# Turning v on TensorE by two transposes instead of selection matmuls, with its cast on GpSimd, in a linear-attention and soft-MoE kernel

## The chip, the cores and the metric

The kernel runs on one core of a Trainium2 chip. The metric is the time of one launch on the device in microseconds (us); lower is better. The core's engines work side by side, each through its own instructions in the order of the program: TensorE (PE in the profile; PEld is its loading of weights), VectorE (DVE), ScalarE (ACT), GpSimd (POOL) and SyncE (SP), which issues most of the loads. The transfers themselves run on sixteen DMA engines that all the issuing queues share.

## The reference

Two parts follow each other. The first is a linear attention with a decaying state, for a batch B of 4, 8 heads H, 768 tokens S and a head width D of 48:

```python
for t in range(S):
    kt, vt, rt = (k[:, :, t], v[:, :, t], r[:, :, t])
    cur = np.einsum('bhd,bhe->bhde', u[None] * kt, vt)
    y[:, :, t] = np.einsum('bhd,bhde->bhe', rt, state + cur)
    state = w[None, :, :, None] * state + np.einsum('bhd,bhe->bhde', kt, vt)
```

Its result becomes x, 3072 tokens of width 384. The second part is a soft mixture of experts with 8 experts of 4 slots each and an inner width of 1024. The logits are x @ phi. A softmax over the tokens mixes tokens into slots, each expert applies its w1, a maximum with zero and its w2 to its four slots, and a softmax over the slots mixes the results back into tokens. All inputs and the output are float32.

## The kernel before

**Units and iterations.** A unit m is one batch and two heads, so there are 16. A unit's 768 tokens are worked in two halves of three chunks of 128 tokens; the main loop runs i from -5 to 31, and iteration i belongs to unit mu = i // 2, half i % 2 ("odd" is the second half). The recurrence is rewritten in chunks: within a chunk, scores of keys against queries are masked to the past and multiplied by v; between chunks a state is carried in Mb. The powers of the decay w are multiplied into k and r beforehand, by tables W that tt (VectorE) and ex (ScalarE's exp) make during the first iterations.

**How k and r arrive.** In SBUF a partition holds six consecutive tokens (J = 6) of each head. scale multiplies k (j = 0) or r (j = 1) of unit m by its table and casts to bfloat16, on VectorE for m = 0 and on GpSimd for all others; three buffers kr_t take the results. t_pe transposes these six blocks on TensorE into T0 or T1, and t_evac on ScalarE copies them to kT or rT, putting the tokens in order as it does. b_pe and b_evac turn kT back, so that kn has tokens on partitions.

**How v arrives.** v is loaded by half: a partition holds three consecutive tokens (JV = 3) of each half, in pieces of 576 bytes. v_cast casts a unit to bfloat16 (v_bf), on GpSimd for m = 0 and on ScalarE for the others. v_pe brings a half's tokens in order by nine matmuls with the stationary selection matrix Q3, which v_evac copies out of the bank Vb as vn:

```python
for c in range(L):
    for j in range(JV):
        o = C * c - j + JV - 1
        O(pe.matmul(Vb[:, c * P2:(c + 1) * P2], Q3[:, o:o + C], vb[:, :, g, j, :],
                    start=(j == 0), stop=(j == JV - 1)))
```

**Order within an iteration.** The function O keeps the order written in the program for every engine. Iteration i issues a_pe and mask_f for half i+1 (scores, and VectorE's mask into AT), y_pe and y_evac for half i, v_pe and v_evac for half i+2, m_pe and z_evac for half i+1 (state, and VectorE's Z and dv), then VectorE's prod_f in even iterations or b_pe and b_evac in odd ones. GpSimd gets scale(mu+3, 0) in odd iterations and scale(mu+2, 1) in even ones. Then follow t_pe and t_evac of unit mu+2 (k in even, r in odd iterations), and v_cast(mu+2) in even ones. For batches that are complete, route adds the logits and the dispatch in three parts. mask_f reads the bank Ab, z_evac reads Mb, and prod_f reads T1 and kT.

**Loads.** SyncE issues k, r and v of batch 0 in pieces of two heads, then batch 1 likewise, phi, and batch 2 in three large transfers. One half of the first k piece is issued by ScalarE. Batch 3 reuses batch 0's buffer and is issued at iteration 3. The expert weights are issued by GpSimd at points of the loop given by a dictionary from iteration to number of transfers, the first right after a small copy that waits for k of batch 3:

```python
W_AT = {12: 1, 13: 1, 14: 1, 15: 1, 17: 1, 19: 1, 20: 1, 22: 1, 23: 1, 25: 1, 26: 5}
...
if i == min(W_AT):
    O(pool.tensor_copy(guard[:], raw_of(0, B - 1)[:, 0:1]))
```

The eight w1 matrices have memory of their own (w_all in the profile). Those of w2 go where batches 1 and 2 lay. After the loop come the last routing, the experts (L628 for w1, L665 for w2) and the output in eight transfers.

Of the kernel before, what the change touches and what calls it, by code (L numbers as in the profile page):

```python
# [9 lines left out]
def kernel(  # L10
# [13 lines left out]
    B, H, S, D = r.shape  # L24
    C = 128
    nC = S // C
# [17 lines left out]
    JV = T // C  # L44

    f32 = mybir.dt.float32
    bf = mybir.dt.bfloat16
# [11 lines left out]
    wk = ctx.enter_context(tc.tile_pool(name="wk", bufs=3))  # L59
# [14 lines left out]
    def raw_of(which, b):  # L74
        return raw[b % NR][:, which * RW:(which + 1) * RW]
# [3 lines left out]
    Ab = psb.tile([128, 2, 512], f32, name="Ab")  # L79
# [3 lines left out]
    Vb = psb.tile([128, 512], f32, name="Vb")  # L83
# [17 lines left out]
    phi_f = late[:, 128:128 + nM * ES]  # L101
# [7 lines left out]
    O(act.dma_start(out=wu3[0:4, :, 0:D], in_=w.rearrange("(q e) d -> q e d", e=2)))  # L109
    O(act.dma_start(out=wu3[4:8, :, 0:D], in_=u.rearrange("(q e) d -> q e d", e=2)))  # L110
    O(dve.memset(warm, 0.0))
    O(dve.memset(one_f, 1.0))
    zt = cst.tile([128, nQ, 3, P2], f32, name="zt")
    O(dve.memset(zt[:], 0.0))

    def load_kr(which, src, b, h0, h1):
        O(sp.dma_start(out=raw_of(which, b).rearrange("p (h x) -> p h x", h=H)[:, h0:h1, :],
                       in_=src[b, h0:h1].rearrange("h (p j) d -> p h (j d)", j=J)))

    def load_v(b, h0, h1):  # L120
        O(sp.dma_start(out=raw_of(2, b).rearrange("p (h x) -> p h x", h=H * G)[:, h0 * G:h1 * G, :],
                       in_=v[b, h0:h1].rearrange("h (g p j) d -> p (h g) (j d)", g=G, j=JV)))

    def load_batch(b, step, h=0):
        for h0 in range(h, H, step):
            load_kr(0, k, b, h0, h0 + step)
            load_kr(1, r, b, h0, h0 + step)
            load_v(b, h0, h0 + step)
# [1 line left out]
    O(sp.dma_start(out=RK[:, 0, :], in_=k[0, 0].rearrange("(p j) d -> p (j d)", j=J)))  # L130
    load_kr(1, r, 0, 0, 2)
    load_v(0, 0, 2)
    load_batch(0, 2, 2)
    load_batch(1, 2)
    O(sp.dma_start(out=phi_f, in_=moe_phi.rearrange("(p mo) s -> p (mo s)", mo=nM)))
    load_batch(2, H)

    def load_w(n, y0=0, y1=nF):
        if n < E:
# [18 lines left out]
    Q3 = cst.tile([128, QW], bf, name="Q3")  # L158
# [17 lines left out]
    ident = cst.tile([128, 128], bf, name="ident")  # L176
# [21 lines left out]

    tt(0, 0)
    tt(1, 0)  # L200
    spread(Vb, P2, H * D)
    ex(0, 0)
    ex(1, 0)
    wT = cst.tile([128, nQ], f32, name="wT")
# [18 lines left out]
    phi_b = acc[:].bitcast(bf)[:, 0:nM * ES]  # L223
    guard = cst.tile([128, 1], f32, name="guard")
    st = {}


    def scale(m, j):
# [28 lines left out]
        O(dve.tensor_copy(kn[:].rearrange("p c t -> p (c t)"), T0[:, 0:S]))  # L257

    def prod_f(m):
        pr = wk.tile([128, S], bf, name="prod", bufs=2)  # L260
        st["prod", m] = pr
        O(dve.tensor_mul(pr[:].rearrange("p (s j) -> p s j", j=J),  # L262
                         T1[:, 0:S].rearrange("p (j s) -> p s j", j=J),
                         st["kT", m][:].rearrange("p (s j) -> p s j", j=J)))


    def v_cast(m):
        b, q = divmod(m, nQ)
        vb = wk.tile([128, 2, G, JV, D], bf, name="v_bf", bufs=2)
        st["vb", m] = vb  # L270
        out, src = vb[:].rearrange("p h g j d -> p (h g j d)"), raw_of(2, b)[:, 2 * q * G * JV * D:2 * (q + 1) * G * JV * D]
        if m == 0:
            O(pool.tensor_copy(out, src))
        else:
            O(act.copy(out, src))  # L275


    def at(i):
        m, g = divmod(i, G)
        b, q = divmod(m, nQ)  # L280
        return m, b, q, g, b * G + g

    def v_pe(i):
        m, b, q, g, n = at(i)
        vb = st["vb", m]
        for c in range(L):
            for j in range(JV):
                o = C * c - j + JV - 1
                O(pe.matmul(Vb[:, c * P2:(c + 1) * P2], Q3[:, o:o + C], vb[:, :, g, j, :],  # L289
                            start=(j == 0), stop=(j == JV - 1)))  # L290

    def v_evac(i):
        vn = wk.tile([128, L, 2, D], bf, name="vn", bufs=3)
        st["v", i] = vn
        O(act.copy(vn[:].rearrange("p c e d -> p (c e d)"), Vb[:, 0:L * P2]))  # L295

    def a_pe(i):
        m, b, q, g, n = at(i)
# [168 lines left out]
            xt_ev(*ch[s])  # L467

    pend = []
    W_AT = {12: 1, 13: 1, 14: 1, 15: 1, 17: 1, 19: 1, 20: 1, 22: 1, 23: 1, 25: 1, 26: 5}  # L470
    T_AT = {-4: [(tt, 0, 1), (tt, 1, 1), (ex, 0, 1), (tt, 0, 2)], -3: [(ex, 1, 1), (ex, 0, 2)],
            -1: [(tt, 1, 2), (ex, 1, 2)], 0: [(tt, 0, 3), (ex, 0, 3)], 1: [(tt, 1, 3), (ex, 1, 3)]}
    Z_AT = {-3: 0, -1: 1, 1: 2, 2: 3}
# [25 lines left out]
    for i in range(-5, nH):  # L499
        mu, odd = divmod(i, 2)  # L500
# [10 lines left out]
        if 0 <= i < nH:  # L511
            y_pe(i)
            y_evac(i)
        if 0 <= i + 2 < nH:
            v_pe(i + 2)
            v_evac(i + 2)
        if 0 <= i + 1 < nH:
            m_pe(i + 1)
            z_evac(i + 1)
# [30 lines left out]
        if i in Z_AT:  # L550
            q = Z_AT[i]
# [12 lines left out]
        if i == 6:  # L564
            for mi in range(nM):
                for j in range(nM):
                    o = C * mi - j + nM - 1
# [3 lines left out]
                                start=(j == 0), stop=(j == nM - 1)))  # L571
# [123 lines left out]
    i = 0  # L695
# [44 lines left out]
```

The softmax here doesn't subtract the row's maximum and nothing guards it: scores larger than these inputs give would overflow.

## Time and profile before

| what | value |
|---|---|
| median of 13 runs | 121.8 us (121.13 to 122.4) |
| the profiled execution | 122.4 us |
| span of its instructions | 120.6 us |
| TensorE busy | 104.2 us (86%) |
| VectorE busy | 96.6 us (80%) |
| ScalarE busy | 83.8 us (69%) |
| GpSimd busy | 59.5 us (49%) |
| GpSimd's scalings of k and r (L233) | 30, 1425 ns each |
| v's selection matmuls (L289) | 288, 18.6 us busy |
| v's copies out of Vb (L295) | 32, 418 ns each |
| v's casts on ScalarE (L275) | 15, 677 ns each |
| v's cast on GpSimd (L273) | 1, 1027 ns |
| issue of one weight transfer on GpSimd (L140) | 591 ns |

The times come from one execution recorded by the hardware profiler. Matmuls overlap one another, so a matmul's mean duration is longer than the distance between two of them, and a TensorE that is busy all the time need not be at its peak; the distance between starts in the timeline is the better price. In the list of costly groups each row gives the line of the code, the engine and operation, what is written from what, the shape, the count, the busy time with the mean of one, and the idle time of the engine just before these instructions. The page's slices cut the span into 40 equal parts and show the busy share of each in tenths. In the rows of DMA queues stand the packets, the megabytes and the share of sixteen engines' time: q1 carries what SyncE issues, q0 what GpSimd issues.

### The profile page before, as it was taken

To read this page: it belongs to the slowest core of one execution; us is meant where nothing else is said; L and a number is where in the kernel's file an instruction comes from. 1 tells how busy PE (TensorE), PEld (TensorE's weight loads), DVE (VectorE), ACT (ScalarE), POOL (GpSimd) and SP (SyncE) were. 2 spreads that over 40 slices of the span, in tenths; PEclk is the share of its full clock that TensorE was granted. 3 is DMA by queue.
4 is the path that set the end of the run, shared out by engine and by line. 5 is a ranking of instruction groups with operands and counts; after the bars stand their busy time and mean duration, and the time that the engine had idled before them with its cause. 6 is when DMAs were issued, how large, how long until landed. Compare 5 with 4: busy or idle time off the path is not lost.

```text
span 120.6 us, 4336 instructions
## 1 busy us (share of the span) xinstructions
PE 104.2 (86%) x1797; PEld 83.8 (70%) x1797; DVE 96.6 (80%) x187; ACT 83.8 (69%) x183; POOL 59.5 (49%) x70
## 2 busy tenths in 40 slices
PE   5896997799999999999999999999998998896000
PEld 1356886588888888888888898898785596783000
DVE  6889989999999999899999899999964430399000
ACT  4359668799788898988997997999792520298000
POOL 7337713599999999978686596101000000011100
PEclk9999999999999999999999999999999999999855
DMA  3999999999999999999999999999999998179991
GB/s 104 309 326 374 376 371 370 310 381 372 294 368 384 359 244 215 211 216 215 216 215 216 213 216 215 215 219 211 219 204 225 214 205 154 21 273 383 412 428 69
DMA packets 20798, 31.79 MB, mean 264 GB/s; under 512 B 1130, under 2 KB 17899, under 8 KB 20651
## 3 DMA queue, kind: packets, MB, share of 16 engines
q0 software_dynamic: 2960, 15.34, 56.6%
q1 hardware_dynamic: 17648, 16.03, 39.8%
q8 instruction: 14, 0.23, 0.7%
q10 hardware_dynamic: 170, 0.15, 0.4%
q14 instruction: 6, 0.04, 0.1%
HBM read 39.38 MB, written 4.72 MB: 366 GB/s over the span
## 4 chain that ended last, share of the span: by engine, by line
PE 51%; DMA 21%; DVE 11%; ACT 4%; issue 3%; POOL 2%; POOLq 0%; DVEq 0%; ACTq 0%
DMA raw<-in_moe_w_dram 21%; PE Vb L289 8%; PE T L240 7%; PE Ab L304 5%; PE Yb L357 5%; PE T L252 4%; PE Mb L330 4%; PE Yb L370 3%; DVE raw L691 2%; PE Yb L368 2%; PE Xb L392 2%; PE Xb L385 2%; PE Yb L149 2%; POOL kr L233 2%; DVE prod L262 1%
## 5 line engine op out<-in xcount | busy, mean ns | idle before, releaser
L233 POOL TENSOR_TENSOR kr<-raw,W 128x576 bf16<-128x576 f32 x30 | 42.2, 1425 | 14.3 <-PE T L240 5.1
L309 DVE TENSOR_TENSOR AT<-Ab,mask_ut 128x768 bf16<-128x768 f32 x32 | 30.2, 944 | 0.8 <-PE Ab L304 0.6
L289 PE MATMUL Vb<-v_bf,Q 128*128 128x96 bf16 x288 | 18.6, 213 | 0.0
L240 PE MATMUL T<-ident,kr 128*128 128x128 bf16 x192 | 17.3, 231 | 1.0 <-POOL kr L233 1.0
L289 PEld LDWEIGHTS <-Q 128*128 128x128 bf16 x288 | 16.6, 102 | 1.6 <-issue 0.2
L246 ACT COPY kT<-T 128x768 bf16<-128x768 bf16 x16 | 12.8, 799 | 4.6 <-PE T L240 3.3
L246 ACT COPY rT<-T 128x768 bf16<-128x768 bf16 x16 | 12.8, 800 | 4.3 <-PE T L240 3.6
L262 DVE TENSOR_TENSOR prod<-T,kT 128x768 bf16<-128x768 bf16 x16 | 15.1, 947 | 0.0
L347 DVE TENSOR_TENSOR dv<-vn,Mb 128x288 bf16<-128x288 bf16 x32 | 14.1, 440 | 0.0
L240 PEld LDWEIGHTS <-kr 128*128 128x128 bf16 x192 | 12.7, 103 | 1.8 <-POOL kr L233 1.2
L295 ACT CAST vn<-Vb 128x288 bf16<-128x288 f32 x32 | 13.4, 418 | 0.1
L346 DVE TENSOR_TENSOR Z<-Mb,zt 128x288 bf16<-128x288 f32 (+1 forms) x32 | 12.7, 396 | 0.8 <-PE Mb L334 0.2
L377 ACT CAST x<-Yb 128x288 bf16<-128x288 f32 x32 | 13.1, 409 | 0.2 <-PE Yb L370 0.2
L304 PE MATMUL Ab<-rT,kT 64*128 64x128 bf16 x192 | 11.3, 225 | 1.5 <-DVE AT L309 1.4
L709 POOL DMA_DIRECT2D out_dram<-W x1 | 0.6, 552 | 24.3 <-DVE W L691 24.3
L330 PE MATMUL Mb<-vn,kn 128*128 128x96 bf16 (+2 forms) x80 | 11.6, 245 | 0.0
L357 PE MATMUL Yb<-vn,AT 128*128 128x48 bf16 x192 | 10.4, 186 | 0.1
L275 ACT CAST v_bf<-raw 128x576 bf16<-128x576 f32 x15 | 10.1, 677 | 0.0
L357 PEld LDWEIGHTS <-AT 128*128 128x128 bf16 x192 | 7.1, 97 | 3.4 <-issue 0.2
L370 PE MATMUL Yb<-dv,ident 128*128 128x288 bf16 x32 | 9.3, 290 | 0.2
L143 POOL DMA_DIRECT2D raw<-in_moe_w_dram x10 | 5.5, 557 | 7.6 <-DMA raw<-in_moe_w_dram 4.1
L304 PEld LDWEIGHTS <-kT 64*128 64x128 bf16 x192 | 5.7, 96 | 5.0 <-DVE AT L309 1.2
(143 smaller groups left out, 223.3 us busy)
## 6 DMA issues: line engine op xcount, KB each, us to landing
w_all<-in_moe_w_dram POOLq DMA_DIRECT2D x8, 768.0 KB, 12.9
raw<-in_moe_w_dram POOLq DMA_DIRECT2D x7, 768.0 KB, 18.0
raw<-in_v_dram SPq DMA_DIRECT2D x12, 288.0 KB, 6.6
raw<-in_r_dram SPq DMA_DIRECT2D x8, 288.0 KB, 5.8
raw<-in_k_dram SPq DMA_DIRECT2D x2, 1152.0 KB, 10.7
raw<-in_r_dram SPq DMA_DIRECT2D x2, 1152.0 KB, 9.4
raw<-in_k_dram SPq DMA_DIRECT2D x7, 288.0 KB, 6.0
out_dram<-raw POOLq DMA_DIRECT2D x1, 1536.0 KB, 6.7
```

Of the source, the lines that this page charges most:

```text
L233: O(eng.tensor_mul(kr[:, j].rearrange("p j (h s) -> p j h s", s=64)[:, :, :, 0:D], src, W[j][:, q].rearrange("p j (h d) -> p j h d", h=2)))
L240: O(pe.transpose(bank[:, x * C:(x + 1) * C], kr[:, j, x, :], ident[:]))
L246: O(act.copy(t[:].rearrange("p (s j) -> p s j", j=J), bank[:, 0:S].rearrange("p (j s) -> p s j", j=J)))
L262: O(dve.tensor_mul(pr[:].rearrange("p (s j) -> p s j", j=J), T1[:, 0:S].rearrange("p (j s) -> p s j", j=J), st["kT", m][:].rearrange("p (s ...
L289: O(pe.matmul(Vb[:, c * P2:(c + 1) * P2], Q3[:, o:o + C], vb[:, :, g, j, :], start=(j == 0), stop=(j == JV - 1)))
L295: O(act.copy(vn[:].rearrange("p c e d -> p (c e d)"), Vb[:, 0:L * P2]))
L304: O(pe.matmul(Ab[:, e, c * C:(c + 1) * C], kT[s, t], rT[s, t]))
L309: O(dve.tensor_mul(AT[:], Ab[:, :, 0:T].rearrange("p e (c t) -> p e c t", c=L), mask_ut[:, None, None, :].to_broadcast([128, 2, L, C])))
L330: O(pe.matmul(o, kn[:, g * L + c, :], vc, start=first, stop=True, skip_group_check=True))
L347: O(dve.tensor_mul(dv[:], st["v", i][:].rearrange("p c e d -> p (c e) d"), Mb[:, 288:288 + 2 * L, None].to_broadcast([128, L * 2, D])))
L357: O(pe.matmul(Yb[:, o:o + D], AT[:, e, c, :], vn[:, c, e, :], start=first, stop=False, skip_group_check=True))
L377: O(act.copy(st["x", n][:, :, q * P2:(q + 1) * P2], Yb[:, 0:L * P2].rearrange("p (c e) -> p c e", c=L)))
```

## The change

v is now loaded exactly like k and r, six consecutive tokens per partition and head, in pieces of 1152 bytes. GpSimd casts units 0 and 4 to 15, ScalarE units 1 to 3; the cast moves from iteration 2m-4 to iteration 2m-5 of the loop, where it stands between the two scalings that GpSimd has there.

v_turn puts a unit in token order in two steps. In the even iteration vt_pe makes twelve transposes (six token positions for each of two heads) into the bank Vb, the second head on partitions from 64 on, and vt_evac copies 112 partitions out in token order as vT. In the odd iteration vn_pe makes six transposes back, 112 columns each, into the same bank, and vn_evac copies both halves out at once. From i = 1 on a turn stands where v_pe stood, before m_pe; up to i = 0 it stands after t_evac and, in odd iterations, b_pe and b_evac. Because partitions 48 to 63 of Vb are never written by a turn, VectorE clears Vb at the start, and the small product at the start that used Vb now uses Ab. The buffers prod and v_bf go from two to one.

The loads of batch 0 from the fifth on are issued later in the program. Ahead of the fifth to the eighth, GpSimd copies one element of the load four earlier into the place where the new load will land, so each waits until that earlier load has landed. The first weight transfer is placed at iteration 11 instead of 12, and all the later ones move by one too.

```diff
     O(dve.memset(warm, 0.0))
+    O(dve.memset(Vb[:], 0.0))
...
     def load_v(b, h0, h1):
-        O(sp.dma_start(out=raw_of(2, b).rearrange("p (h x) -> p h x", h=H * G)[:, h0 * G:h1 * G, :],
-                       in_=v[b, h0:h1].rearrange("h (g p j) d -> p (h g) (j d)", g=G, j=JV)))
+        load_kr(2, v, b, h0, h1)
...
     load_v(0, 0, 2)
-    load_batch(0, 2, 2)
-    load_batch(1, 2)
-    O(sp.dma_start(out=phi_f, in_=moe_phi.rearrange("(p mo) s -> p (mo s)", mo=nM)))
-    load_batch(2, H)
+    load_kr(0, k, 0, 2, 4)
...
-    spread(Vb, P2, H * D)
+    spread(Ab[:, 0, :], P2, H * D)
...
+    def first_of(x):
+        q, t = divmod(x, 3)
+        return raw_of(t, 0)[0:1, 2 * q * J * D:2 * q * J * D + 1]
+
+    for x in range(4, 3 * nQ):
+        q, t = divmod(x, 3)
+        if x < 8:
+            O(pool.tensor_copy(first_of(x), first_of(x - 4)))
+        load_kr(t, (k, r, v)[t], 0, 2 * q, 2 * q + 2)
+    load_batch(1, 2)
+    O(sp.dma_start(out=phi_f, in_=moe_phi.rearrange("(p mo) s -> p (mo s)", mo=nM)))
+    load_batch(2, H)
...
-        pr = wk.tile([128, S], bf, name="prod", bufs=2)
+        pr = wk.tile([128, S], bf, name="prod", bufs=1)
...
+    Vh = Vb[:].bitcast(bf)
+    PV = 64 + D
+
     def v_cast(m):
         b, q = divmod(m, nQ)
-        vb = wk.tile([128, 2, G, JV, D], bf, name="v_bf", bufs=2)
+        vb = wk.tile([128, 2, J, D], bf, name="v_bf", bufs=1)
...
-        if m == 0:
+        if 0 < m < nQ:
+            O(act.copy(out, src))
+        else:
             O(pool.tensor_copy(out, src))
-        else:
-            O(act.copy(out, src))
+
+    def vt_pe(m):
+        vb = st["vb", m]
+        for j in range(J):
+            for e in range(2):
+                O(pe.transpose(Vh[64 * e:64 * e + D, j * C:(j + 1) * C], vb[:, e, j, :], ident[:]))
+
+    def vt_evac(m):
+        vT = wk.tile([128, S], bf, name="vT", bufs=1)
+        st["vT", m] = vT
+        O(act.copy(vT[0:PV].rearrange("p (s j) -> p s j", j=J),
+                   Vh[0:PV, 0:S].rearrange("p (j s) -> p s j", j=J)))
+
+    def vn_pe(m):
+        vT = st["vT", m]
+        for c in range(nC):
+            O(pe.transpose(Vh[:, c * C:c * C + PV], vT[0:PV, c * C:(c + 1) * C], ident[0:PV, 0:PV]))
+
+    def vn_evac(m):
+        vn = wk.tile([128, nC, 2, D], bf, name="vn", bufs=3)
+        for g in range(G):
+            st["v", m * G + g] = vn[:, g * L:(g + 1) * L]
+        O(act.copy(vn[:].rearrange("p c e d -> p (c e) d"),
+                   Vh[:, 0:S].rearrange("p (x s) -> p x s", s=64)[:, :, 0:D]))
+
+    def v_turn(m, back):
...
+        if back:
+            vn_pe(m)
+            vn_evac(m)
+        else:
+            vt_pe(m)
+            vt_evac(m)
...
-    W_AT = {12: 1, 13: 1, 14: 1, 15: 1, 17: 1, 19: 1, 20: 1, 22: 1, 23: 1, 25: 1, 26: 5}
+    W_AT = {11: 1, 12: 1, 13: 1, 14: 1, 16: 1, 18: 1, 19: 1, 21: 1, 22: 1, 24: 1, 25: 5}
...
-        if 0 <= i + 2 < nH:
-            v_pe(i + 2)
-            v_evac(i + 2)
+        if i > 0:
+            v_turn(mu + 2, odd)
...
-        if odd == 0 and 0 <= mu + 2 < nU:
-            v_cast(mu + 2)
+        if i <= 0:
+            v_turn(mu + 2, odd)
+        if odd and 0 <= mu + 3 < nU:
+            v_cast(mu + 3)
```

More of the change, by code (lines that the diff above doesn't have):

```diff
@@ L264, in prod_f @@
                          st["kT", m][:].rearrange("p (s j) -> p s j", j=J)))
+    Vh = Vb[:].bitcast(bf)
+    PV = 64 + D
     def v_cast(m):
         b, q = divmod(m, nQ)
-        vb = wk.tile([128, 2, G, JV, D], bf, name="v_bf", bufs=2)
+        vb = wk.tile([128, 2, J, D], bf, name="v_bf", bufs=1)
         st["vb", m] = vb
-        out, src = vb[:].rearrange("p h g j d -> p (h g j d)"), raw_of(2, b)[:, 2 * q * G * JV * D:2 * (q + 1) * G * JV * D]
-        if m == 0:
+        out, src = vb[:].rearrange("p h j d -> p (h j d)"), raw_of(2, b)[:, 2 * q * J * D:2 * (q + 1) * J * D]
+        if 0 < m < nQ:
+            O(act.copy(out, src))
+        else:
             O(pool.tensor_copy(out, src))
-        else:
-            O(act.copy(out, src))
+    def vt_pe(m):
[19 more added lines that the diff above has]
+    def v_turn(m, back):
+        if not 0 <= m < nU:
+            return
+        if back:
+            vn_pe(m)
+            vn_evac(m)
+        else:
+            vt_pe(m)
+            vt_evac(m)
     def at(i):
@@ L281, in at @@
         return m, b, q, g, b * G + g
[L283 to L295, printed above, removed]
     def a_pe(i):
```

## The prediction

> **What bounds the kernel now.** I read the page's slices and queue rows first, then the chain of waits, then GpSimd's timeline, then the end of TensorE's.
>
> ```profile
> DMA  3999999999999999999999999999999998179991
> GB/s 104 309 326 374 376 371 370 310 381 372 294 368 384 359 244 215 211 216 215 216 215 216 213 216 215 215 219 211 219 204 225 214 205 154 21 273 383 412 428 69
> ...
> q0 software_dynamic: 2960, 15.34, 56.6%
> q1 hardware_dynamic: 17648, 16.03, 39.8%
> ```
>
> The transfers never stop from 3 us to about 100 us: first r, k and v on q1 (about 370 GB/s), then the expert weights on q0 (215 GB/s written). The change of rate, 355 to 237 GB/s between 41 and 44 us in one-microsecond windows, is where weights take over. The packets put q0's first at 41.9 us and leave 0.65 us of input work after it, so the inputs alone would end at 42.55.
>
> ```profile
> 77.73 0.28 issue
> 78.02 25.43 DMA raw<-in_moe_w_dram
> 103.48 0.24 PE Xb L665
> 104.26 0.43 DVE W L676
> ```
>
> The chain of waits ends through the last weight, landed at 103.48; only the output stage, 17.1 us, follows. But TensorE is close behind:
>
> ```profile
> PE Xb L665 <- DMA raw<-in_moe_w_dram: 0.8, 2, 0.5
> ```
>
> From 95 us on it waits 0.8 us in all. So no earlier weight can gain more than about 0.8 us unless attention shortens too, while any later one costs in full. When do weights start? GpSimd's timeline:
>
> ```profile
> 23.77 1.42 POOL L233 TENSOR_TENSOR kr<-raw,W 128x576 bf16<-128x576 f32 x1 [1.41 <-ACT W L197]
> 25.12 0.21 POOL L554 MEMSET ones<- 128x128 bf16 x1
> 25.26 0.78 POOL L556 MEMSET Le<- 128x384 bf16 x2
> 26.00 13.73 POOL L233 TENSOR_TENSOR kr<-raw,W 128x576 bf16<-128x576 f32 x10
> 39.65 0.21 POOL L576 COPY guard<-raw 128x1 f32<-128x1 f32 x1
> 39.77 0.75 POOL L140 DMA_DIRECT2D w_all<-in_moe_w_dram  x1
> ```
>
> Ten scalings without a gap (1.373 us each) stand between 26.0 us and the first weight's issue at 39.77. GpSimd is far ahead of the loop there (TensorE is in iteration 9, the issue belongs to 12), so the issue time is GpSimd's own throughput. Its first packet comes 2.1 us later, just before the inputs run out. That junction is the sensitive place.
>
> Attention itself is paced by VectorE:
>
> ```profile
> 30.00:40.00 10.00, 9.92 (x196) 8.34 (x192) 10.00 (x19) 8.18 (x19) 10.00 (x10) 1.00 1.07 350
> ...
> 40.00:50.00 10.00, 9.87 (x203) 8.44 (x197) 9.84 (x19) 8.75 (x21) 9.69 (x10) 1.00 1.08 254
> ```
>
> The columns are PE, PEld, DVE, ACT, POOL. VectorE and GpSimd are both full from 30 to 40 us; a pair of iterations takes VectorE 4.42 us (two masks of 0.87, Z, dv, kn, prod, by their starts).
>
> **What the Trainium skill says.** "GPSIMD Engine Reference", section 3.1, gives about 1.8 cycles an element for a tight one-input loop and 2.6 for two inputs, at 1.2 GHz. An estimate from it for 576 elements: 0.86 and 1.25 us. The trace has 1.03 us for the one cast (L273) and 1.41 for the scalings, both 0.17 above, so I take 1.03, or 0.98 start to start. "DMA: Bandwidth & Descriptors", section "Why small descriptors are slow", gives a fixed 3 cycles a packet beside one per 32 bytes: 2x21 against 39 cycles, 7%, for two 576-byte packets against one of 1152. The trace agrees in kind: 29.9 and 54.0 ns mean, 10%. "TensorE: Matmul & The Clock Gate", Part 1, has half rate before sustained work, 107 and 56 ns for 128 columns. Here six L240 transposes take 0.65 to 0.84 us up to 15 us and 0.33 from about 20 on.
>
> **The change part by part.**
>
> *v's packets.* 8192 of 29.9 ns become 4096 of 54.0: 245 - 221 = 24 us over 16 engines, 1.5 us less input time. Inputs end at 42.55 - 1.5 = 41.05.
>
> *The held-back first loads.* The fifth to eighth load wait for four tiny GpSimd copies, each behind the landing of the load four earlier, so four loads share the start instead of eight. The first four (1.18 MB with ACT's half) at 278 to 334 GB/s from 1.9 us end near 5.8; the fifth is issued at about 4.35 (GpSimd's memsets end at 4.1) against 3.60, and 1.2 us later is just in time. I take no hole; bounds 0 to 0.5. On GpSimd the copies also stand before v_cast(0), which now waits for k's second load, landing near 6.3: start near 6.6, as before (6.60). Bounds -0.8 to +1.0.
>
> *Vb's memset.* 0.45 us by zt's 1.02 for 1152 columns; VectorE's 0.42 us idle before 4.60 hides it. Without that cover it costs 0.45.
>
> *Start-up turns.* In iterations up to 0 v's turns stand behind k's and r's. Twelve transposes at the early spacing of 0.12 take 1.45 us between t_pe(0,0), done at 8.05, and t_pe(0,1). Then ACT's new vT copy (0.70, kT's spacing) stands in front of ex(0,1): 9.5 + 0.1 + 0.7 = 10.3 against 8.94. Scaling (1,0), which waited for that exp (9.71), and TensorE's transposes at 11.57 behind it, were the chain. Cost 1.35 us. Bounds: 0.3, if other waits at 12 us already cover it; 2.2, since ex(1,1) also gets a v copy and a cast in front (+2.5) of which 1.4 is covered. VectorE is full from 13 us on, so the shift stays: scaling (3,1) at 25.1, (4,0) at 27.35.
>
> *Casts on GpSimd.* ACT loses 12 casts; GpSimd gains them, in order between scaling (m,0) and (m,1). First effect: v_cast(4) ends at 27.35 + 1.37 + 0.98 = 29.7, but TensorE wants v's turn in iteration 4, before m_pe, at 27.1 + 1.35 = 28.45. Nothing else may pass on TensorE; VectorE's Z waits for m_pe. Cost: 1.3 us, on VectorE about 1.4. Bounds 0.5 to 2. Afterwards GpSimd needs 3.73 us a pair against 4.42, and with weight issues (0.59 each) at most 4.9, fed from that gain; I find every later cast and scaling on time.
>
> *First weight.* Moved from iteration 12 to 11, it passes one scaling, (8,1). Ahead of it from (4,0): nine scalings and five casts, 9 x 1.373 + 5 x 0.98 = 17.3 us. Issue: 27.35 + 17.3 + 0.1 = 44.8 us, first packet at 46.9. With the inputs done at 41.05 the engines stand still 5.8 us. Less the 1.5 saved, the last weight lands 4.3 us late, at 107.8. Later weights are issued about two transfers ahead (at most 4.9 us a pair for two, 3.7 us each to move), so no second hole.
>
> *Steady turns.* Per pair v's 18 matmuls take 2 x 0.38 = 0.76 us now. New: 12 of 128 columns at 55 ns (L240), 0.67, and 6 of 112 columns, between 42 and 55, 0.29. So +0.29 in even and -0.09 in odd iterations. In even ones m_pe's end already meets Z: at 79.3 us both fall together; at 37.0 there are 0.27 us to spare. Cost 0 in the first pairs, 0.1 to 0.29 in some nine with routing: 1.5 us. ACT: 0.57 + 2 x 0.29 leave, 0.70 and about 0.53 (between xT's 0.37 and kT's 0.70) come: +0.08 a pair, hidden by its idle fifth. kT's copy comes some 0.46 later, hidden by the iteration until b_pe reads it. The single buffers of prod and v_bf cost nothing: prod is written after Z, which waits for its last reader; v_bf is read a pair earlier.
>
> *Sum.* Weights: +4.3. Attention: 1.35 + 1.4 + 1.5 = 4.25, less TensorE's 0.8 slack, 3.45. The later ends it: span 120.6 + 4.3 = 124.9. The profiled execution took 122.4, 1.8 outside the span, and lies 0.6 above the median of 121.8; so the median goes to 126.1.
>
> **The rivals.**
>
> *Attention ends last* (0.22): if VectorE loses 0.3 a pair from iteration 4 on (3.5) and start-up 2.2, 2.2 + 1.4 + 3.5 - 0.8 = 6.3: 128.1. For: even iterations have no room left. Against: the pairs to 40 us have.
>
> *Start-up is absorbed* (0.18): only GpSimd's five casts count. Issue 43.4, hole 4.45, +2.95: 124.7; with the cast at the page's 0.86 us half a microsecond less. If v's half-width turns ran two at a time, that would help here too, not with GpSimd.
>
> *No hole* (0.10, the other side): the smaller packet count decides. If the first weight is issued before 40.4, the hole stays under the 1.5 us saved, and TensorE's 0.8 us is all that can be won: 121.0. It needs GpSimd to find 4.4 us that its gapless stretch from 26 us doesn't show; waits would have to leave before 26. That the move to iteration 11 does what it says, put weights sooner, would be this case.
>
> **How the numbers follow.** My forecast, weights late by 4 to 5, has 0.50: 126.1. The range reaches into both slower rivals: 123.3 (a hole of 3) to 128.3. A measurement tells 0.3%, 0.4 us, from no change: faster 0.07, same 0.03, slower 0.90.
>
> **What would show it.** First weight issue near 44.8 us in GpSimd's timeline; a DMA gap of several microseconds around 41 to 47, in windows; ex(0,1) near 10.3; TensorE waiting about 1.3 us for v_bf in iteration 4; the last weight landing near 107.8; L240's and the new turns' spacing. I am wrong if DMA shows no gap, or if TensorE no longer waits for weights at the end and the time is still longer.

## The result, and the profile after

The changed kernel takes 125.2 us (median of 11 runs, 124.54 to 126.03), against 121.86 us for the kernel before, run beside it. The ratio is 1.0269, with a 95% interval of 1.0244 to 1.0293. The profiled execution took 125.26 us, with a span of 123.5 us against 120.6. That is 2.9 us between the two traces and 3.3 between the medians, since the profiled execution of the kernel before, 122.4 us, lies 0.5 above its median.

First the page of the kernel after: its slices and the queue row of what SyncE issues.

```profile
DMA  4999999999999569999999999999999999169991
GB/s 115 278 274 306 378 392 380 385 392 383 389 382 390 184 82 216 215 216 213 214 217 214 215 212 217 220 210 215 217 217 212 211 210 173 20 232 383 404 438 72
...
q1 hardware_dynamic: 13552, 16.03, 37.5%
```

There is a hole where the kernel before had none: slices 13 and 14 (from 0), about 40 to 46 us, moved 184 and 82 GB/s. Before it the inputs run faster than they did (380 to 392 GB/s from slice 5 on), except in slices 1 to 3, where they run slower. q1 has 4096 packets fewer, as the change says.

The same place in one-microsecond windows of the kernel after. The columns are the window, its length, TensorE's granted clock, the transfer engines' busy share, and GB/s. The busy share adds up the times of packets, so it can pass 1.

```profile
41.00:42.00 1.00, 1.00 0.60 209
42.00:43.00 1.00, 1.00 0.11 38
43.00:44.00 1.00, 1.00 0.00 0
44.00:45.00 1.00, 1.00 1.17 100
45.00:46.00 1.00, 1.00 0.53 104
```

The inputs run out shortly after 41 us. The 247 KB that move after 41.00 would have taken 0.67 us at the 371 GB/s of the microsecond before, so their bulk ends at about 41.7. The first weight packet comes at 44.38. Then the stream starts slowly: from 44.38 to 46.00 it moved 204 KB, where its later 215 GB/s would have moved 348.

Why so late? GpSimd's timeline of the kernel after:

```profile
26.26 1.40 POOL L244 TENSOR_TENSOR kr<-raw,W 128x576 bf16<-128x576 f32 x1
27.61 0.66 POOL L289 CAST v_bf<-raw 128x576 bf16<-128x576 f32 x1
28.24 2.77 POOL L244 TENSOR_TENSOR kr<-raw,W 128x576 bf16<-128x576 f32 x2
...
38.38 2.77 POOL L244 TENSOR_TENSOR kr<-raw,W 128x576 bf16<-128x576 f32 x2
42.20 0.66 POOL L289 CAST v_bf<-raw 128x576 bf16<-128x576 f32 x1 [1.05 <-issue]
42.80 0.19 POOL L611 COPY guard<-raw 128x1 f32<-128x1 f32 x1
42.93 0.74 POOL L137 DMA_DIRECT2D w_all<-in_moe_w_dram  x1
```

Where ten scalings stood, nine scalings and five casts stand now, and the first weight is issued at 42.93 us instead of 39.77. Two things differ from what was expected: a cast takes 0.66 us (0.63 from start to start), and the last of the five waits 1.05 us. That one is the cast of unit 8. The profile names no releaser for it ("issue"). But it writes the single buffer v_bf, which TensorE reads last for unit 7 in the twelve turns that start from 41.55 us on, and with two buffers the wait is gone (v_bf2 below).

And at the end, in TensorE's waits from 85 us on and in the chain of waits, both of the kernel after:

```profile
PE Xb L700 <- DMA raw<-in_moe_w_dram: 2.9, 3, 2.2
```

```profile
81.40 24.83 DMA raw<-in_moe_w_dram
```

The last weight lands at 106.23, 2.8 us later than the 103.48 before, and TensorE waits 2.9 us for weights where it waited 0.8. The span is 2.9 us longer. The experts' first layer starts at 93.63 against 93.01, so attention ends only 0.62 us later. That is not what sets the end.

### The profile page after: what moved, and what is told of

It reads as the page before. It is cut to its first block, busy times and chain, and to the rows that moved or that the text cites. A ratio compares the mean times of both kernels' runs of the same rounds, so it can differ in the third digit from the quotient of the medians.

```text
span 123.5 us, 4306 instructions
## 1 busy us (share of the span) xinstructions
PE 101.9 (82%) x1797; PEld 79.5 (64%) x1797; DVE 95.9 (78%) x188; ACT 86.8 (70%) x171; POOL 67.6 (55%) x86
## 4 chain that ended last, share of the span: by engine, by line
DVE 28%; DMA 20%; PE 10%; POOL 9%; issue 6%; POOLq 0%; DVEq 0%
DMA raw<-in_moe_w_dram 20%; DVE AT L343 10%; DVE prod L273 6%; DVE dv L381 5%; POOL kr L244 3%; POOL raw L140 3%; DVE kn L268 3%; DVE Z L380 2%; PE Vb L295 1%; POOL v_bf L289 1%; PE T L724 1%; PE T L251 1%; PE T L263 1%; DVE raw L726 1%; PE Ab L338 1%
## 5 line engine op out<-in xcount | busy, mean ns | idle before, releaser
L251 PE MATMUL T<-ident,kr 128*128 128x128 bf16 x192 | 16.6, 225 | 1.8 <-POOL kr L244 1.8
L381 DVE TENSOR_TENSOR dv<-vn,Mb 128x288 bf16<-128x288 bf16 x32 | 14.2, 443 | 0.0
L300 ACT COPY vT<-Vb 112x768 bf16<-112x768 bf16 x16 | 13.0, 813 | 1.0 <-PE Vb L295 0.8
L289 POOL CAST v_bf<-raw 128x576 bf16<-128x576 f32 x13 | 8.6, 660 | 4.3 <-POOL kr L244 2.2
L312 ACT COPY vn<-Vb 128x576 bf16<-128x576 bf16 x16 | 10.7, 667 | 0.1
L391 PE MATMUL Yb<-vn,AT 128*128 128x48 bf16 x192 | 10.3, 185 | 0.1
L295 PE MATMUL Vb<-ident,v_bf 128*48 128x128 bf16 x192 | 8.9, 233 | 1.6 <-ACT v_bf L287 0.9
L268 DVE COPY kn<-T 128x768 bf16<-128x768 bf16 x16 | 8.8, 549 | 0.6 <-PE T L263 0.6
L295 PEld LDWEIGHTS <-v_bf 128*48 128x48 bf16 x192 | 6.1, 108 | 4.8 <-issue 2.2
```

The source lines that it names most:

```text
L251: O(pe.transpose(bank[:, x * C:(x + 1) * C], kr[:, j, x, :], ident[:]))
L295: O(pe.transpose(Vh[64 * e:64 * e + D, j * C:(j + 1) * C], vb[:, e, j, :], ident[:]))
L300: O(act.copy(vT[0:PV].rearrange("p (s j) -> p s j", j=J), Vh[0:PV, 0:S].rearrange("p (j s) -> p s j", j=J)))
L381: O(dve.tensor_mul(dv[:], st["v", i][:].rearrange("p c e d -> p (c e) d"), Mb[:, 288:288 + 2 * L, None].to_broadcast([128, L * 2, D])))
L391: O(pe.matmul(Yb[:, o:o + D], AT[:, e, c, :], vn[:, c, e, :], start=first, stop=False, skip_group_check=True))
```

## The experiments

The theory: *weights late*. The casts on GpSimd put off the first weight's issue, the transfer engines run dry, and the last weight sets the end. Its main rival: *attention late*, the turns and waits on TensorE, VectorE and ScalarE set the end. A smaller question was what the held-back first loads and the larger pieces do. The table gives the medians, the ratio to the kernel before with its interval, and from each trace the first weight's issue, the transfer engines' busy share from 38 to 48 us, the start of the experts' first layer, and TensorE's wait for weights from 85 us on. A busy share of 1.1 there means no hole; 0.76 means that some 3 of the 10 us are missing. Each ratio is to executions of the kernel before that ran beside that kernel (their medians lie from 121.75 to 121.96 us), so it is not quite the quotient of two medians of the table. Each trace is one execution.

| kernel | median, us | ratio | first issue | share 38 to 48 | first layer | wait |
|---|---|---|---|---|---|---|
| before | 121.86 | 1 | 39.77 | 1.10 | 93.0 | 0.8 |
| after | 125.2 | 1.0269 [1.0244, 1.0293] | 42.93 | 0.76 | 93.6 | 2.9 |
| w_sooner | 122.22 | 1.0028 [1.0008, 1.0049] | 39.65 | 1.08 | 93.4 | 1.3 |
| w_later | 125.6 | 1.0324 [1.0253, 1.0395] | 43.75 | 0.67 | 93.1 | 3.6 |
| v_bf2 | 125.58 | 1.0315 [1.0261, 1.037] | 42.83 | 0.76 | 94.4 | 2.3 |
| no_hold | 125.45 | 1.0294 [1.0223, 1.0364] | 42.25 | 0.67 | 93.0 | 3.5 |
| before_gpsimd_casts | 125.6 | 1.0299 [1.0253, 1.0345] | 43.47 | 0.80 | 91.6 | 5.5 |
| act_casts | 129.71 | 1.0652 [1.0616, 1.0689] | 39.01 | 1.08 | 101.8 | 0 |
| act_casts_even | 122.63 | 1.006 [1.0024, 1.0097] | 39.34 | 1.07 | 95.1 | 0 |
| act_casts_even_no_hold | 122.71 | 1.0066 [1.004, 1.0092] | 39.33 | 0.98 | 95.1 | 0 |
| sooner_no_hold | 122.35 | 1.0031 [1.0009, 1.0052] | 40.44 | 0.84 | 94.2 | 0.5 |
| sooner_no_hold_act4 | 122.04 | 1.0022 [1.0002, 1.0043] | 39.78 | 1.00 | 93.6 | 0.7 |
| before_w_sooner | 121.94 | 1.0014 [0.999, 1.0038] | 37.95 | 1.09 | 92.6 | 0.8 |
| before_hold | 123.09 | 1.0098 [1.0063, 1.0133] | 39.28 | 1.10 | 92.5 | 2.2 |

**w_sooner: weights one iteration sooner still.** From the kernel after:

```diff
-    W_AT = {11: 1, 12: 1, 13: 1, 14: 1, 16: 1, 18: 1, 19: 1, 21: 1, 22: 1, 24: 1, 25: 5}
+    W_AT = {10: 1, 11: 1, 12: 1, 13: 1, 15: 1, 17: 1, 18: 1, 20: 1, 21: 1, 23: 1, 24: 5}
```

> The changed kernel with every weight transfer one iteration sooner (the first at iteration 10). The first weight then stands ahead of scaling (8,0) and of the cast of unit 8, which waits 1.05 us. 'Weights late': first issue near 39.8 us, no gap, the last weight about 2.5 us sooner; TensorE's end is then near 104, so 122.5. 'Attention late': 125 as it is, or worse, since the issues now delay the casts of units 8 to 10.

It measured 122.22 us (its trace is the slowest of its twenty executions, 123.12). Nothing of the computation and nothing of GpSimd's work was taken away; only the place in its queue changed. Its timeline of GpSimd shows the issue ahead of the cast that waits:

```profile
39.65 0.74 POOL L137 DMA_DIRECT2D w_all<-in_moe_w_dram  x1
...
42.00 0.66 POOL L289 CAST v_bf<-raw 128x576 bf16<-128x576 f32 x1 [0.17 <-POOL kr L244]
```

Three of the 3.3 us lost are back. If attention set the end, this edit could not have given them: the first layer starts at 93.4 against 93.6, only 0.2 us sooner. The last weight lands at 104.06 instead of 106.23. That settles the main question.

**w_later: the weights put back where they were.**

```diff
-    W_AT = {11: 1, 12: 1, 13: 1, 14: 1, 16: 1, 18: 1, 19: 1, 21: 1, 22: 1, 24: 1, 25: 5}
+    W_AT = {12: 1, 13: 1, 14: 1, 15: 1, 17: 1, 19: 1, 20: 1, 22: 1, 23: 1, 25: 1, 26: 5}
```

> The changed kernel with every weight transfer one iteration later (the first at iteration 12). On GpSimd the first weight then stands behind one more scaling, (8,1), 1.4 us. Theory 'weights late' (the gap before the first weight sets the end): first issue near 44.3 us instead of 42.93, the gap and the time grow by 1.4 us, to 126.6. Rival 'attention late' (v's turns and GpSimd's stalls set the end, the gap is incidental): TensorE's 2.9 us of waiting for weights at the end shows slack on the other side, so this theory expects at most 0.5 us, 125.2 to 125.7.

It measured 125.6 us, a figure in the rival's range. But the interval of its four executions, 125.0 to 126.8 us, holds the theory's 126.6 as well, so the time alone decides nothing. The trace speaks for the theory: TensorE waits 3.6 us for weights, and the chain of waits ends through the last one (81.89 + 24.33).

The first packet came 0.8 us later than in the kernel after (45.19), yet the last weight landed at the same time, 106.22. In four-microsecond windows w_later is behind by 164 KB at 48 us and still by 152 KB at 104 us, 0.7 us at 215 GB/s: the delay was carried through the whole stream. It vanishes in the last two microseconds. In windows of the kernel after, and then of w_later:

```profile
104.00:105.00 1.00, 1.00 0.65 113
105.00:106.00 1.00, 1.00 0.22 35
```

```profile
104.00:105.00 1.00, 1.00 1.01 181
105.00:106.00 1.00, 1.00 0.69 117
```

In the kernel after the busy share falls to 0.22 before the last weight is in; in w_later it stays at 0.69. Why, these runs don't say. The two traces also differ in TensorE's clock at the start (last section): w_later's has it full, and is the fastest of its four executions. Among executions with a mean granted clock of 0.967 or more, two of w_later took 125.22 and 125.25 us and those of the kernel after 124.54 to 124.87, so like against like the delay costs about 0.6 us, still less than the 1.4 expected. As a test of size this one missed.

**v_bf2: two buffers for v_bf.** Memory for the second comes from a small tile that is laid into a table that is free then.

```diff
-    wu = cst.tile([8, 128], f32, name="wu")
+    wu = LexpT[0:8, 1792:2048].bitcast(f32)
...
-        vb = wk.tile([128, 2, J, D], bf, name="v_bf", bufs=1)
+        vb = wk.tile([128, 2, J, D], bf, name="v_bf", bufs=2)
```

> The changed kernel with two buffers for v_bf (the room comes from putting the small table wu into memory that is free at the start). 'Weights late': the cast of unit 8 no longer waits 1.05 us for TensorE's turn of unit 7, the first weight is issued near 41.9 instead of 42.93, and the time falls by 1.0 us, to 124.2. 'Attention late': no effect, 125.2, since TensorE doesn't wait for that cast.

The wait of the cast of unit 8 is gone: it starts at 41.78 instead of 42.20. But the first packet came at 44.27, only 0.11 us sooner, since in this execution GpSimd reached unit 4 some 0.8 us later. The median, 125.58 against the 124.2 expected, is no better than the kernel after: a miss. All four of its executions had a low mean clock, 0.942 to 0.957. So the 1 us wait is real in the trace, but what it costs by itself isn't shown.

**no_hold: the first loads not held back.**

```diff
-        if x < 8:
-            O(pool.tensor_copy(first_of(x), first_of(x - 4)))
```

> The changed kernel without the four small copies, so that eight loads are in flight from the start as before. 'Weights late': inputs end about 1.3 us sooner (41.3 instead of 42.6), the gap before the first weight grows by as much, and the time stays at 125.2 (within 0.4). Rival 'slow start' (the hold-back at the start is part of the loss): 124 or less. If the first v lands later instead, GpSimd's first cast and all behind it shift by up to 0.5 us.

It measured 125.45 us, within the expected range. The bulk of the inputs ended at about 40.3 instead of 41.6 us (both reckoned at the 389 GB/s of the last full microseconds), so holding back costs some 1.3 us of transfer. Without it the hole was only wider, since the weights were not there to fill it.

**before_gpsimd_casts: the casts alone.** The kernel before, with the casts of units 4 and up on GpSimd and nothing else changed:

```diff
-        if m == 0:
-            O(pool.tensor_copy(out, src))
-        else:
+        if 0 < m < nQ:
             O(act.copy(out, src))
+        else:
+            O(pool.tensor_copy(out, src))
```

> The kernel before with one thing moved: the casts of units 4 to 15 from ScalarE to GpSimd (selection matmuls, small pieces of v and weight iterations as before). 'Weights late': five casts of 0.62 us stand ahead of the first weight, issue near 42.9 instead of 39.77, first packet near 44.4, inputs done at 42.7, so some 1.7 us of gap and a slow first transfer: 124.0, that is 2 us of the change's 3.3. If moving the cast is harmless: 121.9.

It measured 125.6 us, ratio 1.0299: this one part alone loses as much as the whole change, and more than the 124.0 expected, which had no wait for the cast in it. In its timeline of GpSimd the weight now stands behind the same cast, and in TensorE's waits the end waits for weights:

```profile
42.74 0.66 POOL L275 CAST v_bf<-raw 128x576 bf16<-128x576 f32 x1 [0.96 <-POOL kr L233]
...
43.47 0.75 POOL L140 DMA_DIRECT2D w_all<-in_moe_w_dram  x1
```

```profile
PE Xb L665 <- DMA raw<-in_moe_w_dram: 5.5, 4, 3.1
```

The wait is longer than in the kernel after because attention is done sooner here: the first layer starts at 91.6, 1.4 us before that of the kernel before. ScalarE's relief is a gain, but one that the late weights hide.

**act_casts: the casts back on ScalarE.** In the kernel after:

```diff
-        if 0 < m < nQ:
+        if m > 0:
             O(act.copy(out, src))
```

> The changed kernel with the casts of units 4 to 15 given back to ScalarE (only unit 0 stays on GpSimd); turns, loads and weight iterations as in the change. 'Weights late': GpSimd has nine scalings ahead of the first weight, which is issued near 39.5 us, so there is no gap at 42 us and the time falls to about 122.5, unless ScalarE's 0.57 us more a pair slow the loop. 'v's turns are slow' (the transposes and their two copies cost the time): 125 or more, with ScalarE fuller still.

It measured 129.71 us, a clear miss. The first half of the expectation held: first issue at 39.01, no hole, no wait for weights at the end. But attention fell behind by 8 us. The waits of TensorE, and under them those of VectorE, in this kernel:

```profile
PE Vb L295 <- ACT v_bf L287: 8.6, 13, 0.8
```

```profile
DVE Z L380 <- PE Mb L368: 8.4, 12, 1.1
```

Thirteen times TensorE waits for the cast, 0.66 us each. The timelines of ScalarE and TensorE at one of them:

```profile
54.46 0.68 ACT L287 CAST v_bf<-raw 128x576 bf16<-128x576 f32 x1
```

```profile
55.19 0.52 PE L295 MATMUL Vb<-ident,v_bf 128*48 128x128 bf16 x12 [0.72 <-ACT v_bf L287]
```

The cast is the last instruction of an odd iteration on ScalarE, behind the copy of rT (here at 53.77), and its reader the first of the next even one on TensorE. Nothing lies between them. Where GpSimd casts, it runs ahead of the loop, and the place in the program doesn't matter. So this run shows what moving a cast to an engine that keeps in step with the loop costs if its place is not moved too; it is no measure of ScalarE's load.

**act_casts_even: the cast on ScalarE one iteration sooner**, which needs this beside the edit before:

```diff
-        if odd and 0 <= mu + 3 < nU:
+        if (i == -5 or not odd) and 0 <= mu + 3 < nU:
```

> The changed kernel with all casts but unit 0's on ScalarE and half a pair sooner: in the even iteration, behind the copies of that iteration, instead of at the end of the odd one. 'Cast chain' (the run with ScalarE's casts was slow because its cast stood directly ahead of TensorE's turn): TensorE's waits for v_bf (8.6 us there) go, no gap before the weights, 122.3. 'The turns themselves are slow' or 'ScalarE is full': 125 or more, with TensorE still not waiting for weights at the end.

122.63 us, as expected. TensorE no longer waits for the cast or for weights, but the first layer starts at 95.1, 1.5 us later than in the kernel after; from 20 to 38 us ScalarE is busy for 17.1 of 18 us, against 15.5 in the kernel after. All of the 1.5 lies in the loop: from the start of unit 3's prod to that of unit 15's it takes 56.86 us, against 55.35. With act_casts_even_no_hold, the same without the four small copies,

> As act_casts_even, without the four small copies at the start. With the inputs 1.3 us sooner and nothing in GpSimd's way the last weight lands near 102.8, and TensorE's own end decides: 121.2 if the loop is no longer than before (0.5% under before), 122 if the start-up shift of 0.7 us shows.

it measured 122.71, no gain, where 121.2 or 122 was expected. Transfers no longer set the end there, so making them faster gives nothing.

**sooner_no_hold: weights sooner, and loads not held back.** The edits of w_sooner and no_hold together.

> The changed kernel with the weights one iteration sooner and without the four small copies at the start. Both losses on the transfers gone, v's larger pieces still there: inputs end 1.3 us sooner than with the hold-back, so the last weight could land near 102.8; then TensorE, which comes 0.6 us later out of attention, ends it: 121.2 (0.6% under before). If the sooner weights have no room to start (the copy that guards them waits for batch 3's k), 122.2 as with the hold-back.

122.35 us, a miss: equal to w_sooner within the intervals. Windows of this kernel show why the faster inputs gave nothing:

```profile
40.00:41.00 1.00, 1.00 0.36 128
41.00:42.00 1.00, 1.00 0.25 48
```

The inputs ended sooner and the first weight, issued at 40.44, was too late again, since GpSimd reached unit 4 0.6 us later than in the kernel after (scaling (4,0) at 26.85). In no_hold, which has the same start-up, it got there at 25.57, so this is not the edit's doing (TensorE's clock, last section). The last weight landed at 103.81, 0.25 us sooner than in w_sooner, and now attention is right behind it: the first layer starts at 94.2, and TensorE waits only 0.5 us for weights from 85 us on. The expectation had left out both. So the cast of unit 4, for which TensorE waits, went to ScalarE too (sooner_no_hold_act4: the condition becomes 0 < m <= nQ).

> As the run before it, and ScalarE also casts unit 4, for which TensorE waits 0.6 us in iteration 4. If TensorE ends the time there: 0.5 us less than that run, 120.7. If the transfers still end it: no difference (within 0.3).

122.04 us, with the first layer at 93.6, against the 120.7 expected. The 0.3 us to the run before it are not told from nothing by these intervals, and the trace shows why nothing was to be had: at 28.25 TensorE waits 0.59 us for the same v_bf, now from ScalarE, where it waited 0.56 for GpSimd. As in act_casts, the cast stands right ahead of its reader, and from unit 2's prod to unit 3's VectorE takes 5.03 us as it did in the kernel after. So the stall at unit 4 was moved, not removed. By its median this is the fastest of the changed kernels, but not told apart from w_sooner and sooner_no_hold. None beats the kernel before in the mean of its executions; the last section says what TensorE's clock has to do with it.

**before_w_sooner: the kernel before, with the weights of the kernel after.**

```diff
-    W_AT = {12: 1, 13: 1, 14: 1, 15: 1, 17: 1, 19: 1, 20: 1, 22: 1, 23: 1, 25: 1, 26: 5}
+    W_AT = {11: 1, 12: 1, 13: 1, 14: 1, 16: 1, 18: 1, 19: 1, 21: 1, 22: 1, 24: 1, 25: 5}
```

> The kernel before with only the weights moved one iteration sooner, as in the change. Before there is no gap in the transfers, so nothing can be won at the junction: 121.8 (within 0.4). If weights and inputs then share the engines, the inputs of batch 3 land later, but they aren't needed before 45 us.

121.94 us, no difference. Weights that stand ready while the inputs still keep the engines full gain nothing. In this trace the last one landed at 102.89, 0.6 us sooner, and TensorE waited as long for it; but this execution took 121.86 us and that of the kernel before 122.4, so the 0.6 need not come from the edit.

**before_hold: the kernel before, with its first loads held back as in the kernel after.**

```diff
+    for x in range(4, 3 * nQ):
+        q, t = divmod(x, 3)
+        if x < 8:
+            O(pool.tensor_copy(first_of(x), first_of(x - 4)))
...
```

> The kernel before with only the first loads held back by the four small copies. In the kernel before the transfers have no gap, so what the start loses in transfer time (about 1.3 us) goes to the end: the last weight 1.3 us later, of which nothing is absorbed: 123.0. If the start costs nothing: 121.8.

123.09 us, ratio 1.0098: where no hole hides it, holding back costs 1%. In windows of before_hold, whose columns are the window, its length, the five engines with their instructions, clock, busy share of the transfers and GB/s:

```profile
6.00:10.00 4.00, 3.96 (x32) 2.71 (x30) 3.77 (x5) 2.59 (x7) 1.33 (x4) 1.00 0.99 298
10.00:14.00 4.00, 1.81 (x31) 1.27 (x29) 3.96 (x7) 3.90 (x8) 4.00 (x3) 1.00 1.02 317
```

and of the kernel before:

```profile
6.00:10.00 4.00, 4.00 (x27) 2.66 (x26) 3.68 (x6) 2.64 (x7) 1.32 (x2) 1.00 1.04 335
10.00:14.00 4.00, 3.04 (x33) 2.25 (x31) 3.96 (x7) 3.89 (x8) 4.00 (x3) 1.00 1.10 378
```

In these 8 us it moved 4 x 37 + 4 x 61 = 392 KB less, 1.0 us at 378 GB/s. The rate is lower by 11 and 16%, the engines' busy share only by 5 and 7%: this looks less like a hole between loads than like slower movement with four loads in flight.

## Why the prediction was right, and where its steps were not

The forecast, 126.1 us, was 0.9 us above the result, and its mechanism is the one that the runs show: GpSimd's casts delay the first weight, the transfers run dry at 41 to 45 us, and the last weight sets the end. The steps, in the prediction's order:

**v's packets, 1.5 us less input time.** Right in kind and rather too small: from 20 to 38 us the inputs moved 387 GB/s against 351, and without the hold (no_hold) they end at about 40.3, 2.2 us before 42.55. But the next step takes 1.3 us of that back: the bulk of the inputs ended at about 41.7, not 41.05, and 0.9 us is left.

**Held-back loads, no hole.** This step failed. It asked whether the fifth load would be issued before the first four had landed, and it was; it did not ask whether four loads move as fast as eight. They don't: before_hold is slower by 1%, 1.2 us, and in no_hold 1.3 us of transfer come back.

**Start-up turns, 1.35 us.** Too large. Twelve half-width turns take 0.77 us early on (8.09 to 8.86), not 1.45, and ScalarE's exp behind them, ex(0,1), starts at 9.67, not 10.3. Scaling (4,0) starts at 26.26, 0.26 later than before, not 1.35. On VectorE, by the start of unit 2's prod, it had cost 0.46 (24.85 against 24.39). Even this differs between executions of the same start-up: w_later has 25.72 and 24.30 (TensorE's clock, last section).

**Casts on GpSimd, 0.98 us each.** The term was mis-sized: 0.63. It came from the one cast in the trace before, 1.03 us, which held a wait (see the last section). "GPSIMD Engine Reference", section 3.1, of the Trainium skill gives two figures, and I took the 1.8 cycles an element. Its other one, a body of 1.03 cycles an element at 1.2 GHz, would be an estimate of 0.49 us, and with the 0.17 that I had found above the page's figure 0.66: what the trace has.

**v_cast(4), a stall of 1.3 us.** Right in kind, half in size. The timelines of TensorE and then of VectorE in the kernel after:

```profile
28.32 0.52 PE L295 MATMUL Vb<-ident,v_bf 128*48 128x128 bf16 x12 [0.60 <-POOL v_bf L289]
```

```profile
29.25 0.36 DVE L380 TENSOR_TENSOR Z<-Mb,zt 128x192 bf16<-128x192 f32 x1 [0.53 <-PE Mb L368]
```

TensorE waits for the cast as predicted, 0.60 us, and VectorE loses 0.53.

**Every later cast on time.** Wrong once: the cast of unit 8 waited 1.05 us for v_bf. The prediction dismissed the single buffer because its reader is a pair of iterations earlier. GpSimd had run further ahead than that. In before_gpsimd_casts, with two buffers that are each read in two iterations, a wait of 0.96 stands at the same cast. From unit 10 on every cast waits again, 0.39 to 0.72 us, but none of these stands ahead of the first weight, and TensorE waits for none of them.

**First weight's issue at 44.8, packet at 46.9, hole 5.8 us, last weight 4.3 us late.** Measured 42.93, 44.38, about 2.7, and 2.8. The difference at the issue: start 1.1 sooner, five casts 1.8 less, the wait 1.05 more. The packet came 1.45 us after its issue, not 2.1. The 2.1 was misread as well, since the packets of the kernel before begin at 42.16 and not at 41.9, which makes it 2.4, and it was taken where the engines were full. The hole is smaller by those 2.5 us and by 0.6 for the inputs' later end. Of the saved transfer 0.9 us is left (42.55 to 41.7), so 1.8 us were to be expected at the last weight; the slow start of the stream adds (348 - 204) / 215 = 0.7. The remaining 0.3 us isn't placed.

**Why the sum came so near.** Three terms were too large, by 1.8 us (casts), 1.1 (start) and 0.65 (packet); against them stand the wait of 1.05, the slow start of 0.7 and the 0.3 not placed, none of which the prediction had. The inputs' later end shortens the hole and the saving alike. So the last weight was forecast 1.5 us too late, not 3.55, because errors cancelled. The median came nearer still, to 0.9: the forecast took off 0.6 us because the profiled execution of the kernel before lay that much above its median, and the profiled one of the kernel after lies on its own. The mechanism was foreseen; that its size came out within 1 us is in good part luck.

**Steady turns, 1.5 us on VectorE.** Wrong in sign. From the start of unit 3's prod to that of unit 15's, in VectorE's timeline, the kernel before takes 55.80 us (28.81 to 84.61), before_gpsimd_casts 54.80 (28.44 to 83.24) and the kernel after 55.35 (29.88 to 85.23). So moving the casts off ScalarE gains 1.0 us and the rest of the change takes 0.55 of it back. On TensorE the turns cost nothing: twelve half-width ones take 0.45 us and six whole ones 0.30 in steady state, 0.75 together, against the 0.76 of the 18 matmuls before.

**Attention 3.45 us late, hidden by the weights.** It is 0.62 late: 0.46 of start-up and 0.61 at unit 4, less the 0.45 gained later. The rival *attention ends last* was wide of the mark. *Start-up is absorbed*, 124.7 us, was nearer to the result than the forecast was, in its time and its step, and its remark that half-width turns might run two at a time fits what the last section shows. *No hole* would have needed an issue before 40.4, and w_sooner, with 39.65, shows that it was right on what decides; but even then the changed kernel is 0.3% slower. The held-back loads have a part in that: among executions with a mean clock of 0.967 or more, four of w_sooner took 121.85 to 122.03 us and five of sooner_no_hold 121.34 to 121.88.

What stays open is why the end of the weight stream is drawn out in one kernel and not in another (w_later). Start-up moves GpSimd's place by up to 1.3 us between traces of the same start-up code (no_hold and sooner_no_hold); it goes with TensorE's granted clock, but no run set that clock, so that it is the cause isn't shown.

## What to carry to other kernels

In these runs an instruction that starts a transfer was as late as everything ahead of it in its engine's queue: when work moves onto such an engine, work out the new time of each issue, and set the issue ahead of work that may wait. A cast that is harmless on an engine running ahead of the loop becomes a stall of its full length on one that keeps in step, unless its place in the program is moved too. A saving in transfer is worth something only if another transfer stands ready to use it (no_hold). And before two single traces are compared, see whether TensorE had the same clock in both.

## What the runs showed of the hardware

**A GpSimd cast and VectorE's scalings hold each other up.** The first cast took 1.03 us in the kernel before, 1.22 in before_gpsimd_casts, 1.20 in no_hold and 0.93 in sooner_no_hold_act4; all later ones 0.65 to 0.70. The timelines of GpSimd and VectorE in the kernel before:

```profile
6.60 1.03 POOL L273 CAST v_bf<-raw 128x576 bf16<-128x576 f32 x1 [2.50 <-DMA raw<-in_v_dram]
```

```profile
6.34 1.89 DVE L233 TENSOR_TENSOR kr<-raw,W 128x576 bf16<-128x576 f32 x2 [0.32 <-ACT W L197]
```

It starts inside VectorE's first scaling, which reads two operands from SBUF. In these four kernels the cast ends 1.28 or 1.29 us after the scalings' start, whenever it began (0.06 to 0.35 us after it): 7.63 - 6.34, 7.37 - 6.09, 7.58 - 6.29, 7.50 - 6.22. That is not a rule: in v_bf2 it began 0.08 us after the scalings' start (6.41 against 6.33) and took 0.66. There VectorE lost more. Its two scalings took 2.02 us in v_bf2, 1.89 in the four, and 1.43 in w_sooner, where the cast came only behind them. "GPSIMD Engine Reference", section 1, says that GpSimd shares its SBUF interfaces with VectorE and contends with VectorE's instructions of two SBUF inputs. These traces agree, though no run was made to isolate it; which of the two waits differs from trace to trace.

**Half-width turns go faster than whole ones.** Twelve with 48 columns of weights, written in turn to partitions 0 and 64 on, take 0.52 us from the first start to the last end (the line at 28.32 above). One lasts 0.22, so their starts lie (0.52 - 0.22) / 11 = 0.027 us apart: 27 ns, where whole transposes are 55 ns apart. "TensorE: Matmul & The Clock Gate", Part 3, says that matmuls at different tile positions run at the same time. Two in the time of one fits that; whether the narrower weights alone would do it was not tried.

**A weight stream into idle engines started slowly.** In the kernel after the first packet came 1.45 us after the issue, with the engines empty; in the kernel before 2.4 us after it (42.16 - 39.77), with them full. But the stream into empty engines moved 204 KB in its first 1.62 us, 126 GB/s, against 215 afterwards. before_gpsimd_casts shows the same: its first packet came at 44.92, and it moved 74 GB/s from 45 to 46 us, 172 in the next and 227 in the third. Whether the idle engines or the single transfer under way make it slow wasn't tested.

**TensorE's clock in start-up differs between executions, and the time goes with it.** The page's row PEclk has the granted clock by slices, in tenths. Of the kernel after, and then of sooner_no_hold:

```profile
PEclk9999599999999999999999999999999999999655
PEclk9999855999999999999999999999999999999755
```

In the first a stretch of half clock lies at about 12.5 to 15.9 us, in the second at 14.2 to 21.1. In the kernel after six transposes of k take 0.82 us inside it (14.64) and 0.50 behind it (17.22). Eight of the fourteen traces have such a stretch; w_sooner, w_later and no_hold have none. In the trace of the kernel before full clock comes late: six transposes still take 0.80 us at 14.06, and 0.50 at 19.97. With the same start-up code, unit 2's prod begins at 24.30 us in w_later, 24.85 in the kernel after and 25.67 in v_bf2 (where only one small table lies elsewhere), at 24.16 in no_hold and 25.48 in sooner_no_hold, and at 24.39 in the kernel before and 23.93 in before_w_sooner. From unit 3's prod to unit 15's the five changed ones take 55.34 or 55.35 us alike.

Of every execution the mean granted clock is on record. Where it was 0.967 or more, sooner_no_hold took 121.34 to 121.88 us (5 of 21 executions) and sooner_no_hold_act4 121.40 to 121.75 (9 of 22); the others took 121.83 to 123.03. The kernel before, run beside them, shows no such difference: 121.86 us in the mean at 0.967 or more, 121.78 below. So with the clock full in start-up these two changed kernels, at 121.6 us in the mean, would be some 0.2% faster than the kernel before. This was found by sorting the executions afterwards; no run was made for it, and what starts such a stretch isn't known.
